# One stated order for all loads, weights staged in the ELU results' buffers, every weight cast on GpSimd: attention with beacons, then an ELU feed-forward, on one Trainium2 core

## The chip, the cores and the metric

The kernel runs on one core of one Trainium2 chip. The metric is the device time of one execution in microseconds, the median of several runs. A profile is one more execution, recorded by the hardware profiler; its span runs from the first to the last recorded instruction, and its own total time is given beside it. Engines: PE is TensorE (PEld its weight loads), DVE is VectorE, ACT is ScalarE, POOL is GpSimd, and SP is the engine that issues most DMAs.

## The reference, cut to what matters

Eight batches of eight heads of causal attention over 576 tokens with 16 beacon keys ahead of them, which all queries see; the output, as 4608 tokens of 512 numbers, goes through two multiplications with an ELU between them.

```python
# B, H, S, Nb, D = 8, 8, 576, 16, 64;  w_in 512 x 2048, w_out 2048 x 512
k_all = np.concatenate([beacon_k, k], axis=2)
v_all = np.concatenate([beacon_v, v], axis=2)
scores = np.matmul(q, k_all.transpose(0, 1, 3, 2)) / np.sqrt(D)
scores = np.where(causal, -1e9, scores)        # beacons are never masked
a = softmax(scores)
attn = np.matmul(a, v_all)
x = attn.transpose(0, 2, 1, 3).reshape(B * S, H * D)
h = x @ w_in
g = np.where(h > 0.0, h, np.exp(np.minimum(h, 0.0)) - 1.0)
out = g @ w_out                                # 4608 x 512, float32
```

## The kernel before, in words

**Attention** is done in 32 pairs of heads (n = 4b + hp, four pairs to a batch). For each pair, `load_pair` (L228) brings k and q in float32 by one DMA each, and the pair's beacon keys by a third. `cast_pair` (L238) turns them into bf16: k on DVE, with a second small cast for the beacons (L246), q on POOL (L242). `do_T` transposes both on PE into PSUM, `do_kT` and `do_qT` copy the result to SBUF on DVE, `do_SC` (L321) multiplies the scores in four units, `do_exp` (L329) exponentiates each unit on ACT, `do_mask` (L336) zeroes the triangles on POOL, and `do_AV` (L353) multiplies with v for three ranges of the queries. v is widened by 64 columns of ones, so that the sums of the softmax come out beside the result; `do_rec` (L364, L366) takes their reciprocal on ACT by a logarithm and an exponential, and `do_scale` (L373) writes the product, on DVE, into the transposed activations xT. v comes a batch at a time in five pieces (`load_v`, L251 and L255) and is cast on DVE (L260).

**The feed-forward** runs over nine tiles of 512 tokens, in 16 steps each. `do_mm1` (L384) multiplies 128 columns of w_in with the tile: four matmuls, called a group here. `do_e` (L391) exponentiates on ACT, `do_clamp` (L395) limits to 1 on POOL, `do_join` (L399) subtracts 1 and takes the larger of that and h on DVE, into a buffer gt. The second multiplication (`do_mm2`, L407) has four blocks of tokens of four quarters each, again four matmuls a quarter; `do_osb` (L413) copies a block out of PSUM on DVE, and `do_store` (L417) stores it. Both weights are loaded in 16 pieces of 128 x 512 float32 (`load_w`, L270) and cast to fp16 once (`cast_w`, L275), even pieces on DVE and odd ones on POOL. A first multiplication of steps 4f to 4f + 3 needs the w_in pieces 4f to 4f + 3, and a quarter f of the second needs the w_out pieces 4f to 4f + 3.

**Buffers.** PSUM: two for scores, one for AV, two for the first multiplication (also used by the transposes of batch 0), one for the second (also by half of the AVs of batch 0). SBUF: 4 + 4 for k and q as loaded, 5 for v, 34 for gt, and 8 under the name e, which the exponentials of the ELU and the weights as loaded share.

**What sets the order.** The kernel writes its instructions in an order that a planner (`Plan`, `run`) works out when the program is built. Every step is an `add` with an engine, a key, a duration, the steps it waits for, and buffers that it takes and gives back. The planner plays the program through: an engine that is free takes the ready step of the smallest key whose buffers are free, and on PE only steps within a window of 8 above the smallest key still open. A load is two steps, an issue on SP (planned at 0.1 us) and a transfer on one DMA resource (0.8 us for a k or q, 1.5 for a piece of v, 0.7 for a weight), and 2 us more until it can be used. At run time nothing is chosen anew: each engine and each queue runs its instructions in the order written, and waits at each for the semaphores of what it needs.

**Keys.** `place(b, a)` is 32(b - 1) + 8a: a batch has 32 units, a pair 8. Loads of q and k have 30 below their pair's place (batch 0: from -50 on), v 1.8 pairs into the batch before, w_in from place(0, 2) on, one a unit, and w_out from place(1, 1) on, one each 1.2 units. Tile p has the keys 32p + 2 + 2i for the first multiplication, and the second of tile p lies 33 units behind its first, in between the steps of tile p + 1.

Of the kernel before, what the change touches and what calls it, by code (L numbers as in the profile page):

```python
# [10 lines left out]
FP32 = mybir.dt.float32  # L11
# [4 lines left out]
P = 128  # L16
# [10 lines left out]
class Plan:  # L27
# [16 lines left out]
    def run(self):  # L44
# [15 lines left out]
        while n_left:  # L60
# [37 lines left out]
            assert events, [o.key for o in self.ops if o.seq not in done][:10]  # L98
# [20 lines left out]
def kernel(  # L119
# [68 lines left out]

    konst = ctx.enter_context(tc.tile_pool(name="konst", bufs=1))
# [4 lines left out]
    gpool = ctx.enter_context(tc.tile_pool(name="gpool", bufs=34))  # L194
# [15 lines left out]
    NE = 8  # L210
    with tc.tile_pool(name="psum", bufs=1, space=bass.MemoryType.PSUM) as psum:
        slots = {
            "sc": 2, "av": 1, "hps": 2, "ops": 1, "et": 2, "rl": 2, "e": NE, "gt": 34, "osb": 3,
            "ks": 4, "qs": 4, "kb": 2, "qb": 2, "vst": 5,
        }
        plan = Plan(slots, {"PE": 8.0})
# [6 lines left out]
        def load(key, dur, fn, deps=(), take=()):  # L223

            issue = add("SP", key, 0.1, fn, deps=deps, take=take)
            return add("DMA", key, dur, None, deps=[issue], lat=2.0)

        def load_pair(n, is_k):  # L228
# [3 lines left out]
            nc.sync.dma_start(  # L232
                out=t[0:SP_], in_=src[b, 2 * hp:2 * hp + 2].rearrange("h (p g) d -> p h (g d)", g=G))
            if is_k:
                nc.sync.dma_start(
                    out=t[SP_:SP_ + NB, :, 0:D], in_=beacon_k[b, 2 * hp:2 * hp + 2].rearrange("h n d -> n h d"))

        def cast_pair(n, is_k):  # L238
            t = f32s[n, is_k]
# [5 lines left out]
            if is_k:  # L245
                eng.tensor_copy(out=o[SP_:SP_ + NB, 0], in_=t[SP_:SP_ + NB, :, 0:D])  # L246
# [16 lines left out]
        def load_w(which, i):  # L263
            wst = wsts[which, i] = melt.tile([P, 512], FP32, tag="e", name="wst", bufs=NE)
# [132 lines left out]
        def do_join(tt, fc):  # L397
            gt = gts[tt, fc] = gpool.tile([P, TTS], FP16, tag="gt", name="gt")
# [27 lines left out]

        def plan_loads(n):
            b, hp = divmod(n, HP)
            for i, is_k in enumerate((True, False)):
                tag = "ks" if is_k else "qs"  # L430
                key = place(b, hp) - 30 if b else -50 + 5 * hp
                got = load(key + 0.1 * i, 0.8, partial(load_pair, n, is_k), take=[tag])
                qk_in[n, is_k] = add(
                    "DVE" if is_k else "POOL", place(b, hp - 0.9), 0.95 if is_k else 1.6,
                    partial(cast_pair, n, is_k), deps=[got], take=["kb" if is_k else "qb"], give=[tag])

        def plan_v(b):
            for jc in range(NKC):
                key = -49 + 3 * jc if b == 0 else place(b - 1, 1.8 + 0.4 * jc)
# [96 lines left out]
        for p in range(NTT + 1):  # L536
            plan_tile(p)
# [29 lines left out]
```

## Time and profile before

| what | value |
|---|---|
| median of 3 runs | 416.9 us (416.56 to 418.6) |
| the profiled execution | 418.49 us |
| its span | 416.8 us |
| busy: PE, DVE, ACT, POOL | 368.5, 292.1, 277.4, 186.2 us |
| chain that ended last | PE 72%, DMA 12%, DVE 9%, SP's queue 3% |
| read from and written to HBM | 37.22 MB and 9.44 MB |

How to read what follows: the slices of the page give busy tenths of 40 equal parts of the span. In the view by windows each engine has its busy us and, in brackets, its number of instructions; then come the granted clock of PE (1.00 is full speed), the mean busy share of the 16 DMA engines, and GB/s. In a timeline each entry has its start, its length, engine, line, operation, output <- inputs and count, and in square brackets the idle time of its engine ahead of it with what ended that. In the groups, busy us and mean ns of one stand behind the bar, then the idle time ahead and its releasers.

### The profile page before, as it was taken

What the parts mean: (1) busy time and instruction counts of PE and PEld (TensorE: products, weight loads), DVE (VectorE), ACT (ScalarE), POOL (GpSimd) and SP (SyncE); (2) the same over time, 40 slices, a digit from 0 to 9 for tenths busy, and PEclk for the clock granted to TensorE, in tenths of its full rate; (3) what the DMA queues carried; (4) which work ended last, traced back from release to release, by engine and by line L of the source; (5) the groups of instructions that cost most, each with busy time, mean ns of one, the idle gap of its engine ahead of it and who ended that gap; (6) DMA issues with size and microseconds to landing.
All of it is one profiled execution on the core that took longest, in us unless ns stands there. A gap on an engine that the chain in (4) does not pass through costs nothing.

```text
span 416.8 us, 8380 instructions
## 1 busy us (share of the span) xinstructions
PE 368.5 (88%) x2944; PEld 197.4 (47%) x2944; DVE 292.1 (70%) x593; ACT 277.4 (67%) x561; POOL 186.2 (45%) x358
## 2 busy tenths in 40 slices
PE   2626473878999999999999999999999999999996
PEld 1414231444555555555555555555555554444442
DVE  5837367787888897798779877978686655444431
ACT  2828445778888778888888788788787873333310
POOL 1516245564655445545555555444444443333310
PEclk9956566899999999999999999999999999999999
DMA  8989999822722373237334622210000001010102
GB/s 209 293 204 267 259 292 299 187 75 66 194 84 83 92 185 93 83 112 174 91 92 139 158 83 84 84 54 28 27 27 26 28 26 52 26 52 25 52 25 101
DMA packets 63338, 47.21 MB, mean 113 GB/s; under 512 B 42304, under 2 KB 54592, under 8 KB 63296
## 3 DMA queue, kind: packets, MB, share of 16 engines
q1 hardware_dynamic: 63296, 46.68, 40.3%
q8 instruction: 23, 0.38, 0.4%
q14 instruction: 19, 0.16, 0.1%
HBM read 37.22 MB, written 9.44 MB: 112 GB/s over the span
## 4 chain that ended last, share of the span: by engine, by line
PE 72%; DMA 12%; DVE 9%; SPq 3%; issue 2%; ACT 1%; POOL 1%; DVEq 0%
PE ops L407 28%; PE hps L384 27%; PE av L353 9%; PE sc L321 5%; DMA wst<-in_moe_w_in_dram 4%; DMA st<-in_k_dram 4%; DMA vst<-in_v_dram 3%; DVE gt L399 2%; SPq L232 2%; PE tr L291 2%; DVE xT L373 1%; DMA wst<-in_moe_w_out_dram 1%; PE tr L295 1%; DVE v L260 1%; DVE kT L302 1%
## 5 line engine op out<-in xcount | busy, mean ns | idle before, releaser
L384 PE MATMUL hps<-xT,w_in 128*128 128x512 f16 x576 | 146.6, 386 | 8.1 <-DVE gt L399 8.1
L407 PE MATMUL ops<-w_out,gt 128*128 128x512 f16 x576 | 145.6, 379 | 0.1
L395 POOL TENSOR_SCALAR e<-e 128x512 f32<-128x512 f32 x144 | 90.9, 635 | 107.7 <-ACT e L391 103.1
L399 DVE SCALAR_TENSOR_TENSOR gt<-e,hps 128x512 f16<-128x512 f32 x144 | 96.5, 686 | 45.8 <-POOL e L395 44.3
L391 ACT ACTIVATE e<-hps 128x512 f32<-128x512 f32 x144 | 84.3, 595 | 55.4 <-PE hps L384 47.1
L329 ACT ACTIVATE et<-sc 128x736 f16<-128x736 f32 (+3 forms) x128 | 103.7, 856 | 18.1 <-PE sc L321 17.0
L364 ACT ACTIVATE rl<-av 64x240 f32<-64x240 f32 (+2 forms) x192 | 62.4, 325 | 43.9 <-PE av L353 35.1
L336 POOL TENSOR_SCALAR_AFFINE_SELECT et<-et 128x256 f16<-128x256 f16 (+2 forms) x160 | 59.9, 401 | 64.6 <-ACT et L329 62.9
L384 PEld LDWEIGHTS <-w_in 128*128 128x128 f16 x576 | 54.4, 99 | 67.3 <-issue 11.9
L353 PE MATMUL av<-et,v 128*128 128x80 f16 (+3 forms) x704 | 68.4, 241 | 19.6 <-POOL et L336 12.3
L407 PEld LDWEIGHTS <-gt 128*128 128x128 f16 x576 | 52.1, 98 | 60.2 <-issue 6.8
L373 DVE TENSOR_TENSOR xT<-av,rl 64x240 f16<-64x240 f32 (+2 forms) x192 | 67.9, 354 | 13.0 <-ACT rl L366 10.8
L353 PEld LDWEIGHTS <-v 128*128 128x128 f16 (+1 forms) x704 | 51.0, 102 | 46.5 <-issue 25.4
L321 PE MATMUL sc<-qT,kT 64*128 64x80 bf16 (+3 forms) x704 | 37.5, 238 | 9.2 <-ACT et L329 4.6
L302 DVE COPY kT<-tr 128x576 bf16<-128x576 bf16 x32 | 24.2, 756 | 22.5 <-PE tr L295 22.4
L242 POOL CAST st<-st 96x768 bf16<-96x768 f32 x32 | 26.2, 820 | 28.3 <-DMA st<-in_q_dram 20.7
L366 ACT ACTIVATE rl<-rl 128x240 f32<-128x240 f32 (+2 forms) x96 | 34.8, 363 | 3.0
L321 PEld LDWEIGHTS <-kT 64*128 64x128 bf16 x704 | 22.2, 99 | 30.1 <-issue 22.8
L413 DVE COPY osb<-ops 128x512 f32<-128x512 f32 x36 | 24.9, 690 | 16.3 <-PE ops L407 15.8
L306 DVE COPY qT<-tr 128x576 bf16<-128x576 bf16 x32 | 24.1, 753 | 0.5
L242 DVE CAST st<-st 96x768 bf16<-96x768 f32 x32 | 18.7, 586 | 7.5 <-DMA st<-in_k_dram 6.9
L260 DVE CAST v<-vst 128x512 f16<-128x512 f32 (+1 forms) x40 | 20.7, 539 | 4.5 <-DMA vst<-in_v_dram 3.0
(19 smaller groups left out, 91.6 us busy)
## 6 DMA issues: line engine op xcount, KB each, us to landing
st<-in_k_dram SPq DMA_DIRECT2D x32, 288.0 KB, 3.0
st<-in_q_dram SPq DMA_DIRECT2D x32, 288.0 KB, 3.4
out_dram<-osb SPq DMA_DIRECT2D x36, 256.0 KB, 2.0
vst<-in_v_dram SPq DMA_DIRECT2D x24, 256.0 KB, 4.2
wst<-in_moe_w_in_dram SPq DMA_DIRECT2D x16, 256.0 KB, 5.7
wst<-in_moe_w_out_dram SPq DMA_DIRECT2D x16, 256.0 KB, 6.5
vst<-in_v_dram SPq DMA_DIRECT2D x8, 224.0 KB, 3.8
vst<-in_v_dram SPq DMA_DIRECT2D x8, 160.0 KB, 3.7
```

Of the source, the lines that this page charges most:

```text
L242: eng.tensor_copy(out=o[0:SP_].rearrange("p g h d -> p h g d"), in_=t[0:SP_].rearrange("p h (g d) -> p h g d", g=G))
L321: nc.tensor.matmul(out=sc[:, h, o:o + w], lhsT=kT[D * h:D * h + D, P * jc:P * jc + P], rhs=qT[D * h:D * h + D, q0:q0 + w], start=True, sto ...
L329: nc.scalar.activation(out=ets[n][:, :, c0:c0 + w], in_=scs[n, u][:, :, 0:w], func=AFT.Exp, bias=0.0, scale=float(1.0 / (D ** 0.5)))
L336: nc.gpsimd.affine_select(out=et[:, :, c0:c0 + dw], in_=et[:, :, c0:c0 + dw], compare_op=ALU.is_ge, fill=fill0, base=NB if jc == 0 else 0, ...
L353: nc.tensor.matmul(out=av[:, h, q0 - lo:hi - lo], lhsT=v16[0:m, jc, hp, D * h:D * h + 2 * D], rhs=et[0:m, h, c0:c0 + pw], start=(i == 0), ...
L364: nc.scalar.activation(out=rl[mine, 0:w], in_=av[sums, h, 0:w], func=AFT.Ln, bias=0.0, scale=1.0)
L373: nc.vector.tensor_tensor(out=xT[hp][rows, b * S + lo:b * S + hi], in0=avs[n, r][rows, h, 0:hi - lo], in1=rls[n, r][rows, 0:hi - lo], op=A ...
L384: nc.tensor.matmul(out=hps, lhsT=w_in16[:, cc, P * fc:P * fc + P], rhs=xT[cc][:, TTS * tt:TTS * (tt + 1)], start=(cc == 0), stop=(cc == NC ...
L391: nc.scalar.activation(out=e, in_=hpss[tt, fc], func=AFT.Exp, bias=0.0, scale=1.0)
L395: nc.gpsimd.tensor_scalar(out=e, in0=e, scalar1=1.0, scalar2=0.0, op0=ALU.min, op1=ALU.max)
L399: nc.vector.scalar_tensor_tensor(out=gt, in0=es[tt, fc], scalar=1.0, in1=hpss[tt, fc], op0=ALU.subtract, op1=ALU.max)
L407: nc.tensor.matmul(out=ops, lhsT=gts[tt, fc][:, P * t4:P * (t4 + 1)], rhs=w_out16[:, fc, :], start=(fc == 0), stop=(fc == NFC - 1))
```

## The change

- **Loads.** All issues of loads are sorted by key and each is planned behind the one before. A list FIRST states the first 62 or so: the beacon keys of batch 0, its k, q and v interleaved, the first eight pieces of w_in, beacons and first pair of batch 1, the other eight of w_in, the rest of batch 1, and then w_out. Durations in the plan are new: 0.47 us for an issue, 1.15 for a k or q, 1.5 for v, 1.0 for a weight.
- **Beacon keys** come once a batch for all heads, into a buffer of their own, instead of once a pair. The first load of q is issued from ACT's queue.
- **Weights** are loaded into buffers of the pool gt. A buffer there now has room for two ELU results or one piece of a weight, and there are 20 instead of 34; e has 4 buffers instead of 8. All 32 weight casts run on POOL.
- **Plan.** PE's window is 16 instead of 8; the keys of the copies of kT and qT lie 16 lower; the second multiplication's lag and pitch are given by tile (PACES): it begins 21, 29 and 31 units behind the tile's base for the first three tiles and 33, as before, from the fourth on, and the first multiplications of the first three tiles have a pitch of 1.3, 1.7 and 1.8 units instead of 2. Some durations of casts and copies are new.

The core of the diff:

```diff
-        plan = Plan(slots, {"PE": 8.0})
+        plan = Plan(slots, {"PE": 16.0})
...
-            issue = add("SP", key, 0.1, fn, deps=deps, take=take)
+            issue = add("SP", key, 0.47 * n, fn, deps=deps, take=take)
+            issues.append(issue)
...
+        def load_bk(b):
+            t = bks[b] = stage.tile([P, H, D], FP32, tag="bk", name="bk32", bufs=2)
+            nc.sync.dma_start(out=t[SP_:SP_ + NB], in_=beacon_k[b].rearrange("h n d -> n h d"))
...
-            nc.sync.dma_start(
+            eng = nc.scalar if n == 0 and not is_k else nc.sync
+            eng.dma_start(
...
-            wst = wsts[which, i] = melt.tile([P, 512], FP32, tag="e", name="wst", bufs=NE)
+            wst = wsts[which, i] = gpool.tile([P, 512], FP32, tag="gt", name="wst")
...
-            gt = gts[tt, fc] = gpool.tile([P, TTS], FP16, tag="gt", name="gt")
+            if fc % 2 == 0:
+                both = gpool.tile([P, 2, TTS], FP16, tag="gt", name="gt")
+                gts[tt, fc], gts[tt, fc + 1] = both[:, 0], both[:, 1]
+            gt = gts[tt, fc]
...
+        FIRST = ["b0", "k0", "q0", "v0", "v1", "k1", "q1", "v2", "v3", "k2", "q2", "v4", "k3", "q3"]
+        FIRST += [f"i{i}" for i in range(8)] + ["b1", "k4", "q4"] + [f"i{i}" for i in range(8, 16)]
+        FIRST += ["k5", "q5", "v5", "v6", "v7", "v8", "k6", "q6", "v9", "k7", "q7"] + [f"o{i}" for i in range(16)]
+
+        def load_key(name, key):
+            return FIRST.index(name) - 200 if name in FIRST else key
...
-            got = load(key, 0.7, partial(load_w, which, i), take=["e"])
-            eng, dur = ("POOL", 1.0) if i in ON_POOL[which] else ("DVE", 0.45)
-            w_at[which, i] = add(eng, key + 2, dur, partial(cast_w, which, i), deps=[got], give=["e"])
+            got = load(load_key("io"[which] + str(i), 0), 1.0, partial(load_w, which, i), take=["gt"])
+            eng, dur = ("POOL", 0.65) if i in ON_POOL[which] else ("DVE", 0.55)
+            w_at[which, i] = add(eng, key, dur, partial(cast_w, which, i), deps=[got], give=["gt"])
...
-                    key = base + 2 * i
+                    key = base + pitch1 * i
...
+                    key = base + start2 + pitch2 * i
...
-        ON_POOL = range(1, 16, 2), range(1, 16, 2)
+        PACES = [(1.3, 21, 2.5), (1.7, 29, 2.2), (1.8, 31, 2.1), (2, 33, 2)]
+        ON_POOL = range(16), range(16)
...
+        issues.sort(key=lambda i: i.key)
+        for one, two in zip(issues, issues[1:]):
+            two.deps.append(one)
         plan.run()
```

In the names of FIRST, b is a batch's beacon keys, k and q a pair, v a piece of v (five a batch), i a piece of w_in and o a piece of w_out.

More of the change, by code (lines that the diff above doesn't have):

```diff
@@ L97, in run @@
                 tick += 2
-            assert events, [o.key for o in self.ops if o.seq not in done][:10]
+            assert events, (self.slots, [(o.key, o.eng, o.left) for o in self.ops if o.seq not in done][:10])
             now = events[0][0]
@@ L187 @@
     )
+    NG = 20
     konst = ctx.enter_context(tc.tile_pool(name="konst", bufs=1))
@@ L221, with load @@
         qk_in, v_in, v_cast = {}, {}, {}
-        def load(key, dur, fn, deps=(), take=()):
-            issue = add("SP", key, 0.1, fn, deps=deps, take=take)
+        def load(key, dur, fn, deps=(), take=(), n=1):
+            issue = add("SP", key, 0.47 * n, fn, deps=deps, take=take)
+            issues.append(issue)
             return add("DMA", key, dur, None, deps=[issue], lat=2.0)
+        issues = []
+        bks = {}
+        def load_bk(b):
+            t = bks[b] = stage.tile([P, H, D], FP32, tag="bk", name="bk32", bufs=2)
+            nc.sync.dma_start(out=t[SP_:SP_ + NB], in_=beacon_k[b].rearrange("h n d -> n h d"))
         def load_pair(n, is_k):
@@ L245, in cast_pair @@
             if is_k:
-                eng.tensor_copy(out=o[SP_:SP_ + NB, 0], in_=t[SP_:SP_ + NB, :, 0:D])
+                eng.tensor_copy(out=o[SP_:SP_ + NB, 0], in_=bks[b][SP_:SP_ + NB, 2 * hp:2 * hp + 2])
         def load_v(b, jc):
@@ L430, in plan_loads @@
                 tag = "ks" if is_k else "qs"
[L431 to L435, printed above, removed]
+                key = load_key(("k" if is_k else "q") + str(n), place(b, hp) - 30)
@@ L437, in plan_v @@
+                got = load(key, 1.15, partial(load_pair, n, is_k), take=[tag])
+                cast = add(
+                    "DVE" if is_k else "POOL", place(b, hp - 0.9), 0.82, partial(cast_pair, n, is_k),
+                    deps=[got] + ([bk_in[b]] if is_k else []), take=["kb" if is_k else "qb"], give=[tag])
+                qk_in[n, is_k] = cast
+                if is_k:
+                    cast_k[n] = cast
+        cast_k = {}
         def plan_v(b):
             for jc in range(NKC):
-                key = -49 + 3 * jc if b == 0 else place(b - 1, 1.8 + 0.4 * jc)
@@ L440, in plan_v @@
-                got = load(key, 1.5, partial(load_v, b, jc), take=["vst"])
+                key = load_key(f"v{NKC * b + jc}", place(b - 1, 1.8 + 0.4 * jc))
+                got = load(key, 1.5, partial(load_v, b, jc), take=["vst"], n=2 if jc == 0 else 1)
                 v_cast[b, jc] = add(
-                    "DVE", place(b, -0.7 + 0.16 * jc), 0.45, partial(cast_v, b, jc),
+                    "DVE", place(b, -0.7 + 0.16 * jc), 0.56, partial(cast_v, b, jc),
                     deps=[got, last_AV.get(b - 2)], give=["vst"])
@@ L535 @@
                 plan_pair(b * HP + hp)
-        for p in range(NTT + 1):
+        for p in range(NTT):
             plan_tile(p)
+        for op in seconds:
+            op.deps = [joined[d] if isinstance(d, tuple) else d for d in op.deps]
+        issues.sort(key=lambda i: i.key)
+        for one, two in zip(issues, issues[1:]):
+            two.deps.append(one)
         plan.run()
```

46 lines of the change are left out of this document (26 added, 20 removed).

## The prediction

> **What bounds the kernel now.** I read the page of the profile first, the span and its forty slices of 10.4 us.
>
> ```profile
> span 416.8 us, 8380 instructions
> ...
> PE   2626473878999999999999999999999999999996
> ...
> PEclk9956566899999999999999999999999999999999
> ...
> GB/s 209 293 204 267 259 292 299 187 75 66 194 84 83 92 185 93 83 112 174 91 92 139 158 83 84 84 54 28 27 27 26 28 26 52 26 52 25 52 25 101
> ```
>
> From the ninth slice on PE is full and at full clock; before it PE is mostly idle or at half clock, while the loads run at a mean of 260 GB/s (the first seven slices: 1823/7). So there are two kernels: a start that waits, and some 330 us that only PE bounds. Next the busy time by windows (PE, PEld, DVE, ACT, POOL, clock, DMA share, GB/s), split where PE has become full, with three stretches used below.
>
> ```profile
> 0.00:100.00 100.00, 56.69 (x522) 34.47 (x522) 65.14 (x143) 57.56 (x117) 44.35 (x87) 0.78 0.87 223
> 100.00:417.00 317.00, 311.76 (x2426) 162.95 (x2422) 227.00 (x451) 219.82 (x446) 141.85 (x271) 1.00 0.26 79
> 10.00:20.00 10.00, 7.21 (x86) 4.68 (x83) 7.77 (x18) 8.31 (x19) 5.57 (x10) 1.00 1.02 286
> 30.00:40.00 10.00, 7.47 (x71) 5.46 (x70) 8.50 (x19) 7.28 (x19) 6.82 (x15) 0.54 1.04 257
> 100.00:150.00 50.00, 49.97 (x451) 27.39 (x448) 42.39 (x89) 42.56 (x86) 27.21 (x53) 1.00 0.43 119
> ```
>
> After 100 us PE idles 316.8 - 311.8 = 5.0 us in all. To price the start I turn it into PE work done. The same window from 0 to 100 us for four single lines, in this order: L384 (first multiplication), L407 (second), L353 (AV), L321 (scores).
>
> ```profile
> 0.00:100.00 100.00, 18.12 (x60) 6.42 (x60) 0.78 0.87 223
> ...
> 0.00:100.00 100.00, 1.03 (x4) 0.39 (x4) 0.78 0.87 223
> ...
> 0.00:100.00 100.00, 21.39 (x166) 14.06 (x166) 0.78 0.87 223
> ...
> 0.00:100.00 100.00, 12.26 (x184) 7.10 (x184) 0.78 0.87 223
> ```
>
> Work is issued in groups of four matmuls for both multiplications (144 groups each in all), and a pair of heads takes 22 AV and 22 score matmuls. So at 100 us the kernel has done 15 + 1 groups and 166/22 = 7.5 to 184/22 = 8.4, say 8, of the 32 pairs: two batches. The price of a group at full clock stands in the timeline's last entry of PE:
>
> ```profile
> 397.91 15.00 PE L407 MATMUL ops<-w_out,gt 128*128 128x512 f16 x68
> ```
>
> 15.00/17 = 0.882 us a group. After 100 us there are 129 + 143 = 272 groups, 240.0 us; the other 311.8 - 240.0 = 71.8 us belong to 24 pairs, 2.99 us each. All PE work is then 288 x 0.882 + 32 x 2.99 = 349.8 us. By 100 us 16 x 0.882 + 8 x 2.99 = 38.0 us of it are done, so 62.0 us are lost there: 349.8 + 62.0 + 5.0 = 416.8, the span. The question is how much of the 62.0 us the change wins back.
>
> Where they go, from the timelines of POOL, PE and ACT (start, length, instruction, idle time before it and its releaser):
>
> ```profile
> 9.31 1.70 ACT L329 ACTIVATE et<-sc 128x736 f16<-128x736 f32 x2 [7.23 <-PE sc L321]
> ...
> 28.32 0.82 POOL L242 CAST st<-st 96x768 bf16<-96x768 f32 x1 [9.62 <-DMA st<-in_q_dram]
> ...
> 29.55 0.37 PE L353 MATMUL av<-et,v 128*128 128x256 f16 x1 [7.36 <-POOL et L336]
> ...
> 48.42 0.61 POOL L275 CAST w_in<-wst 128x512 f16<-128x512 f32 x1 [8.13 <-DMA wst<-in_moe_w_in_dram]
> ...
> 55.32 3.62 PE L384 MATMUL hps<-xT,w_in 128*128 128x512 f16 x8
> ```
>
> POOL runs in order. At 18.7 us its next instruction casts a q of batch 1 whose load was queued behind eight weights; POOL stands 9.62 us, and the masks of batch 0 stand behind it, so PE stands 7.36 us. At 40 us the same happens with a weight. The plan counts on loads of 0.8 and 0.7 us (288 KB in 0.8 us would be 369 GB/s) with 0.1 us an issue; they land later, and an in-order queue turns each miss into a stall of everything behind it. The first multiplication starts only at 55.3 us.
>
> **The change part by part.** *Loads in one order, with honest durations.* Sizes from the page:
>
> ```profile
> st<-in_k_dram SPq DMA_DIRECT2D x32, 288.0 KB, 3.0
> ...
> vst<-in_v_dram SPq DMA_DIRECT2D x24, 256.0 KB, 4.2
> wst<-in_moe_w_in_dram SPq DMA_DIRECT2D x16, 256.0 KB, 5.7
> ...
> vst<-in_v_dram SPq DMA_DIRECT2D x8, 224.0 KB, 3.8
> vst<-in_v_dram SPq DMA_DIRECT2D x8, 160.0 KB, 3.7
> ```
>
> Batch 0 is 8 x 288 + 3 x 256 + 224 + 160 = 3456 KB, 3.54 MB. Cumulated in the new order (beacons left out): i3 4.6, i7 5.6, k4 and q4 6.2, i15 8.3, q7 11.3, o3 12.3, o15 15.5 MB. At 260 GB/s plus 3 us for the first landing they arrive at 17 (batch 0), 21, 25, 27, 35, 46, 50 and 63 us. The new plan's 1.15, 1.0 and 1.5 us are 256, 262 and 175 GB/s, no faster than the measured mean, so data should be there when its turn comes and the two stalls go. What is late next? Not w_in (35 us) but the engines that prepare PE's work. ACT's groups on the page, with POOL's masks and clamps:
>
> ```profile
> L395 POOL TENSOR_SCALAR e<-e 128x512 f32<-128x512 f32 x144 | 90.9, 635 | 107.7 <-ACT e L391 103.1
> ...
> L391 ACT ACTIVATE e<-hps 128x512 f32<-128x512 f32 x144 | 84.3, 595 | 55.4 <-PE hps L384 47.1
> L329 ACT ACTIVATE et<-sc 128x736 f16<-128x736 f32 (+3 forms) x128 | 103.7, 856 | 18.1 <-PE sc L321 17.0
> L364 ACT ACTIVATE rl<-av 64x240 f32<-64x240 f32 (+2 forms) x192 | 62.4, 325 | 43.9 <-PE av L353 35.1
> L336 POOL TENSOR_SCALAR_AFFINE_SELECT et<-et 128x256 f16<-128x256 f16 (+2 forms) x160 | 59.9, 401 | 64.6 <-ACT et L329 62.9
> ...
> L366 ACT ACTIVATE rl<-rl 128x240 f32<-128x240 f32 (+2 forms) x96 | 34.8, 363 | 3.0
> ```
>
> A pair costs ACT (103.7 + 62.4 + 34.8)/32 = 6.28 us, a batch 25.1. Two batches and the 16 ELU exponentials of tile 0 are 50.2 + 16 x 0.595 = 59.7 us. ACT starts at 9.3 us, and in undisturbed stretches it is busy 8.31 of 10 and 42.56 of 50 us; I take the 0.85 of the second, and 1.0 and 0.70 as ends (0.73 was reached in 30 to 40 us, with stalls on either side).
>
> *The start.* The beacon load goes ahead of k0, and q0 goes to ACT's queue, behind its table load.
>
> ```profile
> 0.80 1.28 ACT L179 ACT_TABLE_LOAD   x1 [0.80 <-PEq L551]
> ...
> 1.25 0.44 SPq L235 DMA_DIRECT2D st<-in_beacon_k_dram  x1
> ...
> 5.42 0.82 POOL L242 CAST st<-st 96x768 bf16<-96x768 f32 x1 [4.05 <-DMA st<-in_q_dram]
> ```
>
> k0 is issued 0.44 us later, q0 at 2.1 us or so. I take 0.4 us, from nothing to 0.8; below nothing is out, since nothing is issued earlier than it was. ACT then starts at 9.7 us. The three beacon issues fewer per batch save 3 x 0.44 us of SP, which counts for nothing: DMA is full behind it, and if that cover went it would be 1.3 us a batch.
>
> *The sum.* Batch 0's attention is through at 9.7 + 25.1/0.85 = 39.2 us, where the first multiplication can start (55.3 now), and two batches plus tile 0 at 9.7 + 59.7/0.85 = 79.9 us: the state that the kernel has at 100 us today. Of the 40.7 us between, PE needs 4 x 2.99 + 16 x 0.882 = 26.1, which leaves 14.6 for the second multiplication of tile 0, moved forward by the new paces (start 21 instead of 33). It needs o0 to o3, cast at about 52 us; in the 12.8 us until then PE gets its share of the 26.1, 8.2, and 4.6 are lost. So 10.0 us of second multiplication are done too, and the work done at 79.9 us is 38.0 + 10.0 = 48.0. Lost: 31.9 instead of 62.0. Behind it I keep the 5.0 us: **349.8 + 31.9 + 5.0 = 386.7 us of span.** The profiled execution took 418.49 us, 1.7 around its span, and the median of the runs is 416.9, 1.6 less; so I forecast 386.8 us.
>
> At the ends: with ACT at 1.0 the state comes at 69.4 us with 38.0 + 8.5 done, lost 22.9, 377.7; at 0.70 it comes at 95.0 us with all 14.1 us of tile 0's second multiplication done, lost 42.9, 397.7.
>
> *All weight casts on GpSimd.* From the view of line L275:
>
> ```profile
> L275 DVE CAST w_in<-wst x8: 428/460/1277, 29.3 to 55.9; 128x512 f16<-128x512 f32 x8
> L275 POOL CAST w_in<-wst x8: 603/610/786, 34.2 to 56.6; 128x512 f16<-128x512 f32 x8
> L275 DVE CAST w_out<-wst x8: 420/524/829, 58.7 to 80.8; 128x512 f16<-128x512 f32 x8
> L275 POOL CAST w_out<-wst x8: 604/608/847, 61.3 to 82.0; 128x512 f16<-128x512 f32 x8
> ```
>
> POOL gains 16 x 0.61 = 9.8 us, DVE loses 16 of 0.46 to 0.52. Up to 79.9 us POOL has 8 q casts of 0.82 (6.6), the masks of 8 pairs (8 x 59.9/32 = 15.0), 32 casts (19.5) and 16 clamps of 0.635 (10.2): 51.3 us from 5.4 us on, a share of 0.69. That is as much as the 6.82 of 10 us it reached between 30 and 40 us; I cost it at nothing, hidden behind ACT, and this is the weakest cover of the sum (first rival). A cast that waits for its load holds masks, clamps and q casts behind it on POOL, and PE and DVE wait for those.
>
> *Staging in the ELU results' buffers*, 20 of double size instead of 34, and 4 buffers for the exponentials instead of 8: 40 halves hold two tiles of 16 and half a third, more than the 34, and with two PSUM buffers at most two or three exponentials are open. Nothing, on both sides; if a load waited for a buffer, the loads chained behind it on SP would move by as much, and the stores with them.
>
> *PE's window of 16 and the earlier kT and qT copies* reorder work whose sum stays: nothing by themselves. What a wrong order of PE would cost is the second rival.
>
> **The rivals.** *POOL becomes the gate.* Its 51.3 us at the 5.57 of 10 that it showed in the undisturbed stretch end at 5.4 + 51.3/0.557 = 97.5 us instead of 79.9: with 52.1 done, lost 45.4, 400.2 us. For it: four kinds of work wait on one in-order queue. Against: POOL's idle time is put down to ACT in the rows above (103.1 of 107.7, 62.9 of 64.6), so it follows ACT and has room.
> The Trainium skill, SBUF — State Buffer, section "SBUF: two separate sides", has a rule that speaks against the change: VectorE in its two-port mode and GpSimd share a port pair as an exclusive lock, and the loser waits for the whole instruction. DVE's casts of k and v are such copies:
>
> ```profile
> L242 DVE CAST st<-st 96x768 bf16<-96x768 f32 x32 | 18.7, 586 | 7.5 <-DMA st<-in_k_dram 6.9
> L260 DVE CAST v<-vst 128x512 f16<-128x512 f32 (+1 forms) x40 | 20.7, 539 | 4.5 <-DMA vst<-in_v_dram 3.0
> ```
>
> By that rule at most 8 x 0.586 + 10 x 0.539 = 10.1 us are added to POOL: 61.4 at its 0.682 end at 95.4 us and give 398.1. The trace bears it out in small only: POOL's casts lie at 603 to 610 ns with single ones at 786 and 847, and it was DVE's that were stretched (428 to 1277).
>
> *The stalls stay under other names.* The chain fixes the order, not the time; a load that waits for a slot, or an early quarter of the second multiplication queued on PE ahead of its weights, stops an in-order queue as today. Then ACT keeps the share of the old start, (57.56 - 1.28)/90.7 = 0.62: the state comes at 9.7 + 59.7/0.62 = 106.0 us with 52.1 done, lost 53.9, 408.7 us. Against it: the plan's new durations are no shorter than the measured ones.
>
> *Slower: the backlog is spent.* Second multiplications are what fills PE while ACT prepares attention; run early, they are missing later, and PE falls to ACT's pace. ACT has 285.2 - 59.7 = 225.5 us left at 79.9 us, and 18.9 us follow the last first multiplication (416.8 - 397.91). The span passes 418.9 if ACT needs until 400.0 us, a share of 225.5/320.1 = 0.70; at 0.69 it is 425.6 us. For it: the old kernel runs with PE and ACT both high. Against: 0.85 with PE full, and from the fourth tile on the new pace has the old lag.
>
> **How the numbers follow.** The forecast's case has 0.68, own range 378 to 398; POOL as the gate 0.16 (0.05 of it by the lock), at 398 to 401; stalls under other names 0.10, at 409; the spent backlog 0.05, of which 0.04 slower and 0.01 about equal; 0.01 is left for a start that is no better at all, which is no change. About 0.5% is what a measurement of this kernel can tell from no change. Faster is 0.68 + 0.16 + 0.10 = 0.94, the same 0.02, slower 0.04. A range of 377 to 402 us holds the first two cases but for 0.04 below it, so 0.80.
>
> **What would show it.** Right: the first L384 matmul at 37 to 42 us; no wait of POOL for a load above 2 us after 18 us; ACT busy over 0.8 between 10 and 75 us; o15 landed near 63 us; second multiplications from 52 to 56 us; PE full from there on with under 6 us idle to the end; clock 1.0 from about 40 us. Wrong: long POOL waits on weights with ACT idle (first rival); PE below 0.97 after 100 us (third rival); a first multiplication no earlier than 50 us (second rival).

## The result, and the profile after

The changed kernel takes 404.6 us (median of 4), the kernel before beside it 417.1 us: a ratio of 0.968 [0.964, 0.973]. That is 12.5 us won where 30 were forecast, and 2.6 us outside the range. The first of the four executions took 933 us, its 128x512 matmuls at a mean of 0.82 to 0.84 us instead of 0.38; it stays out of the ratio, and it is the one that was profiled, so the profile shown here, and every number "after", is of the same kernel run again: 402.2 us (402.09 to 403.28), 0.965 [0.960, 0.969], profiled execution 402.1 us.

The slices of the page, 10.0 us each:

```profile
span 400.4 us, 8289 instructions
...
PE   2766859799998999999999999999999999999996
...
PEclk9989989999999999999999999999999999999999
...
GB/s 221 281 310 231 318 331 239 110 118 188 88 124 136 98 85 140 133 114 86 139 140 106 68 159 108 133 29 27 28 28 28 27 29 26 54 26 35 46 31 100
```

PE reads 9 from the ninth slice on (80 us, with one 8 later), where before it was from the eleventh (104 us); the slices from the second to the eighth are 5 to 9 instead of 2 to 8, and the clock there, 5 to 9 tenths before, is 8 or 9. The loads come in the first seven slices at a mean of 276 GB/s (1931/7; 260 before). The busy times by windows (PE, PEld, DVE, ACT, POOL, clock, DMA share, GB/s):

```profile
0.00:80.00 80.00, 52.12 (x527) 31.64 (x528) 60.16 (x122) 56.81 (x113) 52.76 (x105) 0.95 0.91 255
0.00:100.00 100.00, 71.23 (x683) 41.51 (x684) 75.05 (x152) 71.65 (x144) 63.57 (x123) 0.95 0.84 235
10.00:75.00 65.00, 47.64 (x484) 28.38 (x480) 49.27 (x98) 52.27 (x106) 47.90 (x91) 0.95 0.95 268
100.00:400.40 300.40, 292.81 (x2262) 152.62 (x2260) 215.32 (x426) 205.03 (x417) 133.58 (x251) 1.00 0.27 79
```

And from 0 to 100 us for L393 (first multiplication; L384 before), L419 (second), L362 (AV), L330 (scores):

```profile
0.00:100.00 100.00, 23.13 (x88) 8.19 (x88) 0.95 0.84 235
...
0.00:100.00 100.00, 12.67 (x45) 4.56 (x46) 0.95 0.84 235
...
0.00:100.00 100.00, 19.92 (x198) 13.87 (x198) 0.95 0.84 235
...
0.00:100.00 100.00, 12.78 (x220) 7.58 (x220) 0.95 0.84 235
```

The prediction's account holds: 22 + 11.25 groups and (198 + 220)/44 = 9.5 pairs are 29.3 + 28.4 = 57.7 us of PE work done by 100 us, where the kernel before had 38.0. Lost there: 42.3 us (62.0 before; 31.9 were forecast). Behind it PE idles 300.4 - 292.8 = 7.6 us (5.0 before). 349.8 + 42.3 + 7.6 = 399.7, for a span of 400.4.

The timelines of ACT, PE and POOL, and DVE, at the places where the kernel before stood:

```profile
0.83 0.41 ACTq L243 DMA_DIRECT2D st<-in_q_dram  x1
...
8.94 3.14 ACT L338 ACTIVATE et<-sc 128x736 f16<-128x736 f32 x4 [6.86 <-PE sc L330]
```

```profile
36.09 0.81 PE L393 MATMUL hps<-xT,w_in 128*128 128x512 f16 x3
...
57.57 0.57 PE L300 MATMUL tr<-identb,st 112*128 112x112 bf16 x6 [4.41 <-DVE st L255]
...
58.41 1.91 PE L393 MATMUL hps<-xT,w_in 128*128 128x512 f16 x4
60.12 1.54 PE L419 MATMUL ops<-w_out,gt 128*128 128x512 f16 x4
...
63.68 1.03 PE L419 MATMUL ops<-w_out,gt 128*128 128x512 f16 x4
```

```profile
29.43 0.82 POOL L251 CAST st<-st 96x768 bf16<-96x768 f32 x1
...
50.88 0.82 POOL L251 CAST st<-st 96x768 bf16<-96x768 f32 x1
51.65 1.17 POOL L284 CAST w_out<-wst 128x512 f16<-128x512 f32 x2
52.79 0.61 POOL L404 TENSOR_SCALAR e<-e 128x512 f32<-128x512 f32 x1
53.35 1.17 POOL L284 CAST w_out<-wst 128x512 f16<-128x512 f32 x2
54.49 0.61 POOL L404 TENSOR_SCALAR e<-e 128x512 f32<-128x512 f32 x1
55.05 0.61 POOL L284 CAST w_out<-wst 128x512 f16<-128x512 f32 x1
55.61 0.38 POOL L345 TENSOR_SCALAR_AFFINE_SELECT et<-et 128x224 f16<-128x224 f16 x1
55.94 1.49 POOL L284 CAST w_out<-wst 128x512 f16<-128x512 f32 x2
```

```profile
52.56 4.40 DVE L251 CAST st<-st 96x768 bf16<-96x768 f32 x1
56.99 0.52 DVE L255 CAST st<-bk 16x128 bf16<-16x128 f32 x1
```

POOL's waits of 9.62 and 8.13 us are gone: its q cast at 29.43 follows a mask without a pause. The first multiplication starts at 36.09 us (55.32 before, 37 to 42 forecast). But there is a new stall: DVE's cast of the eighth k, 0.56 us as a rule, takes 4.40 us, PE stands 4.41 us behind it and comes back at about half speed (a group of four in 1.91 and 1.54 us, against 1.04 otherwise). Beside it POOL runs eleven instructions without a gap, from 50.88 to 57.43 us, seven w_out casts among them. Only the last one is stretched (the pair at 55.94 takes 1.49 us for 1.17). In the view of all casts the median stays as before:

```profile
L284 POOL CAST w_in<-wst x16: 607/612/944, 20.1 to 36.9; 128x512 f16<-128x512 f32 x16
L284 POOL CAST w_out<-wst x16: 607/612/940, 51.6 to 70.7; 128x512 f16<-128x512 f32 x16
```

### The profile page after: what moved, and what is told of

Its sections match the earlier page's. It is cut to its first block, busy times and chain, and to the rows that moved or that the text cites. A ratio compares the mean times of both kernels' runs of the same rounds, so it can differ in the third digit from the quotient of the medians.

```text
span 931.6 us, 8289 instructions
## 1 busy us (share of the span) xinstructions
PE 915.7 (98%) x2944; PEld 357.5 (38%) x2944; DVE 283.1 (30%) x577; ACT 283.5 (30%) x561; POOL 193.8 (21%) x374
## 4 chain that ended last, share of the span: by engine, by line
PE 97%; ACT 1%; DVE 1%; DMA 0%; issue 0%; SPq 0%; DVEq 0%
PE ops L419 37%; PE hps L393 37%; PE av L362 13%; PE sc L330 6%; PE tr L300 2%; PE tr L304 2%; DMA st<-in_k_dram 0%; ACT et L338 0%; DVE kT L311 0%; DVE qT L315 0%; ACT rl L373 0%; ACT rl L375 0%; DVE xT L382 0%; DVE osb L425 0%; DVE st L251 0%
## 5 line engine op out<-in xcount | busy, mean ns | idle before, releaser
L419 PE MATMUL ops<-w_out,gt 128*128 128x512 f16 x576 | 371.2, 835 | 0.0
L393 PE MATMUL hps<-xT,w_in 128*128 128x512 f16 x576 | 367.5, 824 | 0.0
L419 PEld LDWEIGHTS <-gt 128*128 128x128 f16 x576 | 97.1, 173 | 201.3 <-issue 198.1
L393 PEld LDWEIGHTS <-w_in 128*128 128x128 f16 x576 | 90.5, 165 | 194.2 <-issue 191.4
L362 PE MATMUL av<-et,v 128*128 128x80 f16 (+3 forms) x704 | 142.4, 399 | 1.2 <-DVE xT L382 1.0
L362 PEld LDWEIGHTS <-v 128*128 128x128 f16 (+1 forms) x704 | 91.3, 159 | 89.9 <-issue 59.9
L330 PE MATMUL sc<-qT,kT 64*128 64x80 bf16 (+3 forms) x704 | 66.5, 370 | 4.3 <-ACT et L338 2.6
L330 PEld LDWEIGHTS <-kT 64*128 64x128 bf16 x704 | 36.5, 136 | 64.9 <-issue 56.7
L375 ACT ACTIVATE rl<-rl 128x240 f32<-128x240 f32 (+2 forms) x96 | 34.8, 363 | 3.0
L300 PE MATMUL tr<-identb,st 96*128 96x96 bf16 (+1 forms) x192 | 29.1, 340 | 6.5 <-DVE st L255 6.5
L300 PEld LDWEIGHTS <-st 96*128 96x128 bf16 (+1 forms) x192 | 24.1, 167 | 18.6 <-issue 10.8
L304 PE MATMUL tr<-identb,st 96*128 96x96 bf16 x192 | 29.3, 343 | 0.0
```

The source lines that it names most:

```text
L300: nc.tensor.transpose(out=tr[0][:, W * g:W * g + m], in_=kb[0:m, g].rearrange("p h d -> p (h d)"), identity=identb[0:m, 0:m])
L330: nc.tensor.matmul(out=sc[:, h, o:o + w], lhsT=kT[D * h:D * h + D, P * jc:P * jc + P], rhs=qT[D * h:D * h + D, q0:q0 + w], start=True, sto ...
L362: nc.tensor.matmul(out=av[:, h, q0 - lo:hi - lo], lhsT=v16[0:m, jc, hp, D * h:D * h + 2 * D], rhs=et[0:m, h, c0:c0 + pw], start=(i == 0), ...
L393: nc.tensor.matmul(out=hps, lhsT=w_in16[:, cc, P * fc:P * fc + P], rhs=xT[cc][:, TTS * tt:TTS * (tt + 1)], start=(cc == 0), stop=(cc == NC ...
L419: nc.tensor.matmul(out=ops, lhsT=gts[tt, fc][:, P * t4:P * (t4 + 1)], rhs=w_out16[:, fc, :], start=(fc == 0), stop=(fc == NFC - 1))
```

## The experiments

The method of all of them is that of the prediction: work done by 100 us, idle time behind it. Each run's times stand beside those of the kernel before, and "side by side" means on the same chip in turn. The first run is the changed kernel itself, shown above.

> The changed kernel as it is, for a profile at full clock. Measured is a span of 401 to 404 us where the sum gave 386.7, so 15 to 17 us more are lost than the sum has. Theory A, the start: two batches of attention and tile 0 are complete at 95 to 97 us instead of 79.9, and PE idles about 5 us behind that. Theory B, spent backlog: that state comes near 80 us and PE idles about 20 us behind it.

It is nearer to the theory of the start: PE idles 7.6 us behind 100 us, not 20, and the last product of batch 1 went into xT at 89.77 us (the row stands with the account of the prediction).

### Where the gain comes from: the loads

**All of the change but the loads**: old load keys and durations, no chain, the old keys of the weight casts, all else as changed.

```diff
-            issue = add("SP", key, 0.47 * n, fn, deps=deps, take=take)
+            issue = add("SP", key, 0.1, fn, deps=deps, take=take)
...
-            return FIRST.index(name) - 200 if name in FIRST else key
+            return key
...
-            two.deps.append(one)
+            pass
```

> Everything of the change but its loads: the old keys, durations (0.8, 0.7 and 0.1 us an issue) and no chain, and the old keys of the weight casts. Its plan is 397 us long, 3 us shorter than the changed kernel's 400. Theory M (the gain is that loads land when the plan says so, and in-order queues no longer stall): 408 to 418 us, most of the gain gone, with waits of POOL or DVE for loads of over 3 us before 80 us. Rival theory P (the gain comes from the casts, the paces or the window of PE): 398 to 403 us.

413.6 us, 0.990 [0.987, 0.993]. From POOL's and PE's timelines:

```profile
34.35 0.83 POOL L251 CAST st<-st 96x768 bf16<-96x768 f32 x1 [15.08 <-DMA st<-in_q_dram]
```

```profile
35.59 1.37 PE L362 MATMUL av<-et,v 128*128 128x256 f16 x6 [13.28 <-POOL et L345]
```

The stall of the kernel before is back, in one piece and larger: a q cast that waits 15.08 us for its load, and PE 13.28 us behind it. The chain of work followed back through the stretch from 9 to 80 us says the same: transfers of loads are 49 us of it in the kernel before, 27 in this run and 10 in the change.

**The loads alone**: order, chain, durations, beacons by the batch, staging in gt; weight casts split, PE's window 8, the old paces and the old keys of kT and qT.

```diff
-        plan = Plan(slots, {"PE": 16.0})
+        plan = Plan(slots, {"PE": 8.0})
...
-            kT = add("DVE", at(-0.5) - URGE, 0.92, partial(do_kT, n), deps=[T, last_kq.get(n - 3)],
+            kT = add("DVE", at(-0.5), 0.92, partial(do_kT, n), deps=[T, last_kq.get(n - 3)],
...
-            qT = add("DVE", at(-0.49) - URGE, 0.77, partial(do_qT, n), deps=[T, last_kq.get(n - 3)],
+            qT = add("DVE", at(-0.49), 0.77, partial(do_qT, n), deps=[T, last_kq.get(n - 3)],
...
-        PACES = [(1.3, 21, 2.5), (1.7, 29, 2.2), (1.8, 31, 2.1), (2, 33, 2)]
-        ON_POOL = range(16), range(16)
+        PACES = [(2, 33, 2)]
+        ON_POOL = range(1, 16, 2), range(1, 16, 2)
```

> The loads alone (with the beacons by batch and the staging in the gt buffers, which go with them): even weight pieces cast on DVE, second multiplications 33 units behind for every tile, PE's window 8, kT and qT at their old keys. Its plan is 405.6 us long. Theory M: 402 to 407 us, so at least 10 of the 15 us. Theory P: over 412.

397.4 us, 0.950 [0.947, 0.953], faster than the whole change, and no transfer is left in the chain from 9 to 80 us. So the loads bring 20 us by themselves, and the other edits together take 5 back (402.2, against 397.4). The beacons by the batch, the staging and q0's queue were in the run before this one too, so they don't do it without the order, the chain and the durations; these three were not taken apart. Which of the other edits lose, the rest of the runs ask.

### POOL and the stalled k cast

**Casts split again**, even pieces on DVE as before: `ON_POOL = range(1, 16, 2), range(1, 16, 2)`.

> The changed kernel with one edit undone: even weight pieces cast on DVE again, odd ones on POOL, as before the change; 9.8 us less on POOL, 8 us more on DVE. If POOL is the gate of the start (my first rival), this is 6 to 9 us faster than the changed kernel. If ACT is the gate (my forecast), it is within 2 us. If DVE is the gate, it is 4 to 8 us slower.

402.3 us, 0.963 [0.959, 0.967], beside 402.2 for the change. Sixteen casts fewer on POOL win nothing, so the sum of POOL's work is not the gate. The stall is gone (no k cast above 1.005 us), and the time isn't better for it; DVE carries the 16 casts instead, and this run can't part the one from the other.

**Old paces** in the change: `PACES = [(2, 33, 2)]`.

> Only the paces undone: pitch 2 and lag 33 for all tiles. My sum had 10.0 us of second multiplication brought forward into the start; if that were so, this is 7 to 10 us slower than the changed kernel. Theory T (block 0 of the second multiplication needs the last ELU result of tile 0, and one PSUM buffer holds back blocks 1 to 3, so at most three groups, 2.6 us, could come forward): 0 to 4 us slower.

403.1 us, 0.963 [0.958, 0.967]: no difference from the change, with a k cast of 3.83 us.

**Planned dependency**: the casts of w_out pieces 2 to 15 wait, in the plan, for the eighth k cast.

```diff
+        for i in range(2, 16):
+            w_at[1, i].deps.append(qk_in[7, True])
```

> The changed kernel with one more dependency: the weight casts o2 to o15 on POOL wait for the cast of the eighth k on DVE, so that POOL has no unbroken run of casts while that cast is due. Plan 400.0 us, as before. Theory L (DVE's 4.40 us cast was held off by POOL's unbroken run, and PE's 4.41 us of idle time and the half clock behind it follow from that): that cast takes under 1.2 us, PE has no gap over 3 us between 20 and 80 us, and the kernel is 3 to 7 us faster than the changed one, 394 to 398. If the start is bounded by ACT whatever DVE does: within 1.5 us.

404.5 us, 0.967 [0.964, 0.971], and the k cast took 4.39 us. A miss, and an instructive one: the dependency exists in the plan alone. No data passes between the two, so no semaphore does, and on the chip POOL ran its casts when it reached them: pieces 2 to 4 from 54.72 us on, while the k cast ended at 57.74.

**Five w_out casts on DVE**, pieces 2 to 6, in the order that the change's plan gave them.

```diff
-            (nc.gpsimd if i in ON_POOL[which] else nc.vector).tensor_copy(out=dst, in_=wsts[which, i])
+            (nc.gpsimd if (which, i) not in {(1, 2), (1, 3), (1, 4), (1, 5), (1, 6)} else nc.vector).tensor_copy(out=dst, in_=wsts[which, i])
```

> The changed kernel with its plan unchanged (400.0 us), but the weight casts o2 to o6 written to DVE's queue instead of POOL's, at the same places of the order. This breaks POOL's unbroken run at 51 to 57 us at run time (the dependency of e6 was one of the plan alone, and at run time POOL ran its casts ahead of the stalled k all the same). Theory L: the cast of the eighth k takes under 1.2 us instead of 4.40, PE's gap of 4.4 us goes, and the kernel is 3 to 6 us faster than the changed one (396 to 399). If the start is bounded by ACT or by DVE's load, DVE's 2.5 us more make it 0 to 2 us slower.

400.5 us, 0.958 [0.955, 0.962], the longest k cast 1.25 us and PE's gap gone. It won 1.7 us where 3 to 6 were expected.

**The loads and all casts on GpSimd** (the loads alone, with `ON_POOL = range(16), range(16)`).

> e4 (the loads alone, 397.4 us) with all weight casts on GpSimd, nothing else. Its plan is 401.4 us, 4 us shorter than e4's. Theory L: slower than e4 by 3 to 7 us (400 to 404), with a k cast of over 3 us on DVE and a PE gap behind it. If the casts only free DVE: 392 to 396.

400.3 us, 0.958 [0.954, 0.962], 2.8 above the loads alone, with the stall on DVE and on PE:

```profile
52.78 5.19 DVE L251 CAST st<-st 96x768 bf16<-96x768 f32 x1
```

```profile
58.58 0.67 PE L300 MATMUL tr<-identb,st 112*128 112x112 bf16 x6 [5.23 <-DVE st L255]
```

So the casts on POOL can hold DVE up (the run without early keys, below, has them all and no stall). The two runs put 1.7 and 2.8 us on a gap of 4 to 5 us, net of what the casts themselves cost on the one engine or the other. That it is less than the gap fits the work done: the run here has lost 2.5 us more than the loads alone by 80 us, and 0.8 more by 100.

### The second multiplication of tile 0

**Tile 0 in halves**: each block's quarters 0 and 1 close their PSUM bank, DVE copies it out, and quarters 2 and 3 are added later. The change's own code stands against the prediction's 10.0 us: a block's last quarter needs ELU results 12 to 15, and blocks 1 to 3 need block 0's only PSUM buffer. The gt pool has 18 buffers here.

```diff
-                    start=(fc == 0), stop=(fc == NFC - 1))
+                    start=(fc == 0 or tt in HALVED and fc == 8), stop=(fc == NFC - 1 or tt in HALVED and fc == 7))
...
+            if tt in HALVED:
+                nc.vector.tensor_tensor(out=osb, in0=opss[tt, t4], in1=osas[tt, t4], op=ALU.add)
+                return
```

> The changed kernel, the second multiplication of tile 0 done in two halves (steps 0 to 7 of all four blocks, copied to SBUF, then steps 8 to 15, added by DVE), so that eight groups instead of three can come ahead of tile 0's last ELU result; 18 buffers in gt instead of 20 to make room. Its plan is 401.2 us, that of the changed kernel with 18 buffers as well. Theory T in its strong form (the missing 7.4 us of second multiplication are the loss): 3 to 5 us faster than the changed kernel. In its weak form (they are only moved, and PE lacks them behind 80 us, while tile 1 waits for batch 1's attention): within 2 us.

399.6 us, 0.956 [0.952, 0.960], 2.6 below the change; but the order moved with it and the stalled k cast went too (1.18 us at most), so this run doesn't say which of the two won it. It has 6 groups of the second multiplication done by 80 us, the change 3.25. Two more without the earlier keys and with the casts split ask it again.

**The loads and the paces** (the loads alone, with the change's PACES), and **the same in halves**:

> e4 (the loads alone, 397.4 us) with the new paces. Second multiplications may start from 21 units on. My sum's term (7 to 10 us more work in the start): 389 to 392. Theory T: at most three groups come forward, 396 to 399.

> e12 with the second multiplication of tile 0 in halves and 18 buffers in gt, so that eight groups can come forward, in a kernel where no k cast is held off. Theory T, strong form: 392 to 394. Weak form (work is only moved; behind 80 us PE lacks it): within 2 us of e12.

399.6 us (398.31 to 400.62), 0.957 [0.954, 0.960], and 397.7 us (396.38 to 398.74), 0.953 [0.949, 0.956], side by side. The paces win nothing over the loads alone, and the halves 1.9 us. Allowed to start sooner, the second multiplication has 4.5 groups done by 80 us in both (the profiled executions), not 11. The permission was lacking, but lifting it brought far less than the 10.0 us.

### The earlier keys of kT and qT

**The loads and the keys** (the loads alone, with the 16 taken off again).

> e4 with the earlier keys of the copies of kT and qT, nothing else; casts split. Its plan is 401.3 us, 4 us shorter than e4's. If the plan's length carries over when nothing stalls: 392 to 395. If the order of DVE matters more than the plan's length: 397 to 403, as e2, which has these keys too.

403.0 us, 0.964 [0.960, 0.967]: 5.6 us lost, with casts split and no stall (longest k cast 0.90 us). By 100 us it has 20 + 6 groups done, the loads alone 24 + 8.

**The change without the earlier keys**:

```diff
-            kT = add("DVE", at(-0.5) - URGE, 0.92, partial(do_kT, n), deps=[T, last_kq.get(n - 3)],
+            kT = add("DVE", at(-0.5), 0.92, partial(do_kT, n), deps=[T, last_kq.get(n - 3)],
...
-            qT = add("DVE", at(-0.49) - URGE, 0.77, partial(do_qT, n), deps=[T, last_kq.get(n - 3)],
+            qT = add("DVE", at(-0.49), 0.77, partial(do_qT, n), deps=[T, last_kq.get(n - 3)],
```

> The changed kernel with only the earlier keys of the copies of kT and qT undone. Its plan is 402.3 us, 2.3 us longer. If these keys cost what e9 showed (5.6 us on top of the loads alone): 396 to 399, though the casts on POOL may still hold off a k. If they cost only where the casts are split: 402 to 405.

395.3 us (394.81 to 395.57), 0.947 [0.944, 0.950], the fastest of all, with all casts on GpSimd and no long k cast (0.90 us). To tell the size side by side, and the place, four more: the keys early for the pairs of the first two batches only (`URGE if n < 8 else 0`), only behind them (`URGE if n >= 8 else 0`), everywhere (the change), and nowhere.

> The change with the kT and qT copies put forward by 16 for the pairs of the first two batches only (n below 8), and at their old keys behind them. If the 7 us that the earlier keys cost are lost in the start (in the traces the work done by 100 us differs, the idle time behind it hardly), this has them: 400 to 403 us. If they are lost later, 394 to 397. If the size of the loss is an accident of the plan's order, with no place of its own, this and the run with the other half lie anywhere between 393 and 405 without adding up.

> The other half: put forward from the ninth pair on only, old keys for the first two batches. Theory of the start: 394 to 397 us, as with no key put forward. Theory of a later loss: 400 to 403. An accident of the order: anywhere between 393 and 405.

> The changed kernel as it is, beside the others on the same chip: 401 to 405 us.

> The change without the earlier keys of kT and qT, beside it on the same chip: 394 to 397 us, 6 to 8 below the changed kernel. If the 7 us between the two came from two calls on different chips, they lie within 2 us here.

| keys early | median us (lowest to highest) | ratio to before | lost by 100 us | idle behind |
|---|---|---|---|---|
| everywhere (the change) | 402.7 (402.15 to 404.14) | 0.966 [0.961, 0.971] | 44.5 | 7.6 |
| first two batches | 403.1 (400.76 to 403.32) | 0.965 [0.960, 0.971] | 43.4 | 5.9 |
| behind them | 397.2 (397.05 to 398.08) | 0.952 [0.947, 0.958] | 39.1 | 7.4 |
| nowhere | 395.5 (394.91 to 395.76) | 0.948 [0.943, 0.953] | 38.6 | 5.7 |

The last two columns are worked out from the profiled executions as above. For the change and for the kernel without early keys, the rows are these two windows, and then L393, L419, L362 and L330 from 0 to 100 us:

```profile
0.00:100.00 100.00, 73.83 (x666) 43.66 (x667) 73.03 (x147) 70.32 (x141) 61.35 (x120) 0.90 0.84 235
100.00:402.40 302.40, 294.84 (x2280) 153.75 (x2278) 217.70 (x431) 206.15 (x422) 135.04 (x254) 1.00 0.26 79
```

```profile
0.00:100.00 100.00, 23.12 (x88) 8.18 (x88) 0.90 0.84 235
...
0.00:100.00 100.00, 11.27 (x38) 3.84 (x39) 0.90 0.84 235
...
0.00:100.00 100.00, 21.80 (x188) 14.89 (x188) 0.90 0.84 235
...
0.00:100.00 100.00, 13.79 (x220) 8.18 (x220) 0.90 0.84 235
```

```profile
0.00:100.00 100.00, 73.50 (x712) 43.71 (x713) 74.32 (x163) 74.46 (x151) 63.41 (x126) 0.95 0.85 237
100.00:393.50 293.50, 287.80 (x2234) 150.86 (x2232) 209.27 (x416) 200.81 (x411) 130.58 (x249) 1.00 0.27 80
```

```profile
0.00:100.00 100.00, 24.08 (x96) 8.98 (x96) 0.95 0.85 237
...
0.00:100.00 100.00, 12.18 (x48) 4.23 (x48) 0.95 0.85 237
...
0.00:100.00 100.00, 21.30 (x208) 15.42 (x209) 0.95 0.85 237
...
0.00:100.00 100.00, 13.93 (x228) 8.43 (x228) 0.95 0.85 237
```

In the change (88 + 38)/4 groups and (188 + 220)/44 pairs are 55.5 us of work; without early keys (96 + 48)/4 and (208 + 228)/44 are 61.4. By this account the two halves add up: early keys in the first two batches cost 4.8 to 5.4 us in the start (43.4 - 38.6, 44.5 - 39.1), and behind them 1.7 us of idle PE (7.4 - 5.7, 7.6 - 5.9). The medians agree on where the loss lies but don't add up so well: 7.6 us for the first two batches alone, 1.7 for the rest alone, 7.2 for both. Each account is one execution: that of "first two batches" is the fastest of its four (400.76 us), that of the change the slowest (404.14), and the two profiles of the change lie 2.2 us apart in the start (42.3 and 44.5).

What happens in the start is seen in part. The products into xT have keys 16 lower already; with the copies 16 lower too, the planner lets the copies of the next pair pass them in DVE's queue. Between 36 and 80 us PE's AVs waited 5.9 us in all for xT in the loads with the keys, and 1.8 us in the loads alone (total, times, longest):

```profile
PE av L362 <- DVE xT L382: 5.9, 5, 1.9
...
PE av L362 <- DVE xT L382: 1.8, 2, 1.2
```

What the earlier copies win against it is less: PE's scores waited 2.4 us for qT instead of 4.2, and the first multiplications 2.8 us for gt instead of 4.3. PE was busy 28.3 of 44 us against 34.8. In the change itself the stalled k cast is part of the same loss: it came with the keys early everywhere or in the first two batches (4.39 us in both runs), and in neither of the others (0.83 and 0.90 us). Such a stall costs 1.7 to 2.8 us, which leaves 4.4 to 5.5 of the 7.2 for the order itself, an estimate; in the loads with the keys, where nothing stalled, it was 5.6. Which single wait carries it was not settled. In the chain from 9 to 80 us DVE has 27 and 25 us in the two profiles of the change, 10 and 19 in the two without early keys.

The run without early keys is also 4.3 us faster, side by side, than the loads with the paces (395.3 and 399.6). Between the two stand only the casts on GpSimd and PE's window of 16; so with the old keys these two together win something, and which of them does was not tried.

## Why the prediction was wrong in size

The direction and the cause of the gain were right. The account of work done, loss in the start and idle time behind it comes within 1.3 us of the span in all of these executions that were profiled; it is little more than bookkeeping, but it says where the miss lies. Its inputs were off, as 400.4 - 386.7 = 13.7 us: 10.4 in the start (42.3 for 31.9), 2.6 behind it (7.6 for 5.0), 0.7 that the account leaves.

- **The loads and the stalls: right.** No wait of POOL for a load above 2 us is left after 18 us, and taking the loads' order out brings them back. The last issue of w_out came at 51.4 us; with the 5.6 us to landing of the page it was there by 57 us, where 63 were forecast.
- **The start: no slower than before.** The load of q0 left ACT's queue at 0.83 us, not at 2.1, beside the table load that I put ahead of it. The first exponential began at 8.94 us, 9.31 before; in the other profiled runs it lay between 8.56 and 9.39, so the 0.4 us that I took aren't seen, and "below nothing is out" was wrong.
- **"Two batches plus tile 0 at 79.9 us", set by ACT at 0.85: not borne out.** ACT's share from 10 to 75 us is 52.27/65 = 0.80. Batch 0 was through at 37.8 us (39.2 forecast), and the last ELU exponential of tile 0 ran at 75.1. But the last product of batch 1 went into xT ten us after the 79.9, and without the early keys five. From DVE's timelines of the two kernels:

```profile
89.77 0.49 DVE L382 TENSOR_TENSOR xT<-av,rl 64x80 f16<-64x80 f32 x2
```

```profile
84.74 0.49 DVE L382 TENSOR_TENSOR xT<-av,rl 64x80 f16<-64x80 f32 x2 [1.28 <-PE hps L393]
```

Counted as PE work it cost little: 64 matmuls of tile 0 and (158 + 184)/44 pairs, 37.4 of the 38.0 us, were done by 80 us. That ACT sets the pace of the start isn't shown: of the chain from 9 to 80 us DVE has 27 of 71 us and ACT 11, 19 and 19 without the early keys, and no run took work off ACT.
- **"So 10.0 us of second multiplication are done too": failed**, and is the first of the two steps that carry the miss. The first one began at 60.12 us, not at 52 to 56, and 13 matmuls, 3.25 groups, were done by 80 us: 2.9 us. Without the early keys it is 16 matmuls, 3.5 us. The rows of L419 from 0 to 80 us, of the change and of the first run without early keys:

```profile
0.00:80.00 80.00, 3.62 (x13) 1.52 (x14) 0.95 0.91 255
...
0.00:80.00 80.00, 5.01 (x16) 1.54 (x16) 0.91 0.97 270
```

By 80 us the change has lost 39.8 us, 7.9 more than the 31.9: 7.1 are second multiplications that weren't done, the rest mostly attention. Another 2.5 go between 80 and 100 us, where the sum had nothing, and where the kernel without early keys loses nothing: its 38.6 are 6.7 above the 31.9, about the 6.5 that are missing of the 10.0. I had taken all of PE's time between 39.2 and 79.9 us that its share of attention and tile 0 left free as time in which a second multiplication could run. What the free time was made of shows in the first run without early keys, from 36 to 80 us:

```profile
36.00:80.00 44.00, 35.29 (x320) 19.35 (x319) 35.35 (x73) 33.51 (x69) 33.32 (x63) 0.94 0.94 268
```

64 + 16 matmuls and (92 + 88)/44 pairs fall in it, 29.9 us of work by the account, in 35.3 us of busy time; the other 8.7 us are idle in pieces, 8.4 of them in 14 waits of at most 1.8 us for what DVE, ACT and POOL prepare. So of the 17.6 us that attention and tile 0 leave by the account, 3.5 went to second multiplications, 5.4 to the same work taking longer than priced (the granted clock is 0.94 on the mean; the rest was not broken down), and 8.7 to these waits. Letting blocks run in halves won 1.9 us, so most of the rest is not for want of a free block; what would fill it stays open.
- **"PE's window of 16 and the earlier kT and qT copies reorder work whose sum stays: nothing by themselves": failed**, the second step. They cost 7.2 us side by side (402.7 and 395.5); in the two profiled executions, whose spans lie 8.9 us apart, 5.9 in the start and 1.9 behind it. The sum of the work did stay; DVE is an in-order queue that others wait for, and an order there has a price. The window of 16 had no run of its own.
- **"All weight casts on GpSimd ... I cost it at nothing": the gate that I feared didn't come, another stall did.** Splitting the casts wins nothing (402.3 for 402.2). But in the change, and in the loads alone with all casts on POOL, POOL's run of casts holds DVE's k cast for 4 to 5 us, worth 1.7 to 2.8 us. I had read the traces of before as bearing out a lock of the port "in small only", because I priced it on POOL's side, 10.1 us; the one that stood was DVE. The Trainium skill, SBUF — State Buffer, section "SBUF: two separate sides", has the pair held for a whole instruction by whoever starts first; the traces agree that the other stands still, and show more than one instruction of waiting: 4.40 us for a cast of 0.56, behind POOL instructions of 0.4 to 0.6 us each. What the runs themselves show is that the stall comes beside POOL's unbroken casts and goes when they are broken up (1.25 us with five of them on DVE); that it is this lock was not tested apart.
- **"Behind it I keep the 5.0 us": 2.6 short**, of which 1.9 go with the early keys.
- **Slips in the working that moved nothing here.** PE reads 9 from the eleventh slice on in the kernel before, not from the ninth (7 and 8 there). The upper end, 377.7, leaves out the free time that is lost before o0 to o3 are cast; by the rule of the sum itself that is 4.2 us, so 381.9. And the rows that give ACT 59.7 us add up to 285.2 over the kernel, where the page has ACT busy 277.4.

The three rivals: POOL as the gate fell (casts split). Stalls under other names did not come in the form I gave them, for no load was late; the one stall there is, the k cast, would be the lock of the first rival from the other side, at 1.7 to 2.8 us where 11.4 were priced. The spent backlog isn't seen, PE idling 5.7 us behind the start without the early keys, for 5.0 before.

The version that beats both kernels is the change without the earlier keys: 395.5 us, 0.948 [0.943, 0.953], and 395.3 the first time.

## What to carry to other kernels

Where in-order queues are filled by a plan, plan the loads at the rate that the trace shows and in one stated order: here a load that came later than planned stopped everything behind it. A step moved forward in the queue of an engine that others wait for isn't free just because the sum of the work stays (here it cost 7.2 us); run it alone before keeping it. And count idle time as usable only if the next work has its inputs and its buffer in just those pieces.

## What the runs showed of the hardware

A VectorE copy can stand still for a whole run of GpSimd instructions. DVE's k cast (float32 to bf16, SBUF to SBUF, 0.56 us) took 4.39 to 4.40 us in three profiled executions of the change and its first half, 5.19, 4.39 and 3.83 us in three other runs, while POOL's casts beside it ran at 0.61 us, stretched to 0.94 at most. It doesn't always stand so long. Without the early keys the same cast met such a run of POOL too, and was done in 0.79 us:

```profile
54.57 1.17 POOL L284 CAST w_out<-wst 128x512 f16<-128x512 f32 x2
55.70 0.92 POOL L404 TENSOR_SCALAR e<-e 128x512 f32<-128x512 f32 x1
56.57 1.16 POOL L284 CAST w_out<-wst 128x512 f16<-128x512 f32 x2
```

```profile
55.36 0.79 DVE L251 CAST st<-st 96x768 bf16<-96x768 f32 x1
```

Here the clamp that follows was the one to wait (0.92 us for 0.61). What decides who gets in was not tried.

PE loses more than the gap: after standing 4.41 us its next groups of four took 1.91 and 1.54 us where they take 1.04 otherwise, at a granted clock of 0.62 in the window of the changed kernel behind it:

```profile
57.00:60.00 3.00, 2.43 (x16) 1.45 (x17) 2.54 (x6) 0.00 (x0) 0.43 (x1) 0.62 1.11 248
```

The Trainium skill, TensorE: Matmul & The Clock Gate, section "HAM oscillation — how this bites in real kernels", warns of idle gaps above some 3.4 us; the trace agrees at 4.41 us. But a single gap that long isn't needed: in the loads with the keys PE was busy 1.4 of the 4 us from 52 to 56, with no gap above 1.91 us, and from 56 to 58 the clock reads 0.50; it reads 0.50 again from 63 to 66 us, where eight matmuls took 3.40 us for 1.89.
